# 32 by 32 tiles of k and q for the third token group, its weights and gates worked on inside the first output product: an mLSTM cell with a SwiGLU block on one core

## The chip, the cores and the metric

The kernel runs on one core of one Trainium2 chip. The metric is device time in microseconds of one execution. Engines are named as in the profile: PE (matrix), PEld (its weight loads), DVE (vector), ACT (scalar), POOL (GpSimd), SP (the sync engine, which here issues nearly all DMAs).

## The reference

Two stages follow each other. The first is an mLSTM cell for 4 batches, 8 heads, 768 tokens and a head size of 40, with a running matrix C and vector n for each head:

```python
m_new = np.maximum(f_gate[:, :, t] + m, i_gate[:, :, t])
f_stab = np.exp(f_gate[:, :, t] + m - m_new)
i_stab = np.exp(i_gate[:, :, t] - m_new)
C = f_stab[..., None, None] * C + i_stab[..., None, None] * np.einsum('bhd,bhe->bhde', vt, kt)
n = f_stab[..., None] * n + i_stab[..., None] * kt
h_tilde = np.einsum('bhde,bhe->bhd', C, qt)
denom = np.maximum(np.abs(np.einsum('bhd,bhd->bh', n, qt)[:, :, None]), 1.0)
y[:, :, t] = sigmoid(o_gate[:, :, t]) * h_tilde / denom
```

The second takes the 3072 rows of 320 values (heads side by side) through a SwiGLU block: `(silu(x @ w_gate) * (x @ w_val)) @ w_out`, with 1536 hidden columns. All arrays are float32, and the three weight matrices come as float64.

## The kernel before

The 768 tokens are cut into six groups (g = 0 to 5) of 128 tokens for all 4 batches, which makes 512 rows for the SwiGLU block. The engines run in parallel, and each executes its instructions in the order in which the program text issues them; nothing reorders them. The author therefore interleaves by hand: the long matrix products of group g are issued in chunks, and between the chunks stand the small steps that prepare group g + 1 and load group g + 2. These lists are the dictionaries `slots` (after each chunk of the hidden product) and `after` (after each chunk of the first output product).

**The hidden product** of a group is 12 chunks (`hidden`, L613). A chunk is ten matmuls into two PSUM banks (L618), then silu on ACT (L623) and a product on DVE (L624), which frees the banks. The pool "gen" has four such banks, so PE can be two chunks ahead of L624.

**The output product** of a group multiplies the hidden values by `w_out`. For groups 1 to 5 it goes batch by batch (`project`, L631). For group 0 it goes by chunks of hidden columns through all four banks at once (`project_all`, L637, matmuls on L641), because `w_out` is still being converted from float64: each two chunks of it are made by ACT (L186, L188), DVE (L195, L196) and an addition on POOL (L203). `convert(14)` to `convert(17)` stand in `after`. When the last chunk is done, ACT copies the four banks to `z_sb` (L628), which has two buffers, and SP stores each (L629).

**The cell** for a group needs k and q with the head dimension on partitions (`kT`, `qT`). Groups 1 and 2 load tokens on partitions (`load`, L113), transpose on PE (`turn`, L287 and L292; 64 transposes for a group) and copy out of PSUM on ACT and DVE (L117, L119). Groups 3 to 5 load 32 by 32 tiles (`load_squares`, L305, 16 DMAs for q and 16 for k, rows of 32 or 8 values) into zeroed tiles `q_sq` (a view of `q_sb`) and `k_sq`, and DVE transposes these tiles in place of PE (`turn_squares`, L314). k with tokens on partitions (`k_sb`) is wanted in any case, for the state's update (`add`, L343).

The **weights** of a group start as a load of running maxima to `w_sb` (L421). Then DVE subtracts (`weights_sub`, L425), POOL masks (`weights_mask`, L430, two instructions for each half P of the heads), and ACT exponentiates (`weights_exp`, L434). POOL multiplies them into v (`weigh_values`, L337). The **output gates** are a sigmoid on ACT (`sig`, L437). Exponential, sigmoid and silu each need a table load on ACT when one follows another.

Where this is for the third group (n = 2), before the change: loads of v, k, q and o stand after chunks 1 and 3 of the first output product, subtraction and masks after chunks 8 and 9, the exponentials, sigmoids and `weigh_values` behind the whole product (so behind the four z copies on ACT), and the transposes after chunks 0 and 1 of the hidden product of group 1. The buffers "raw" (two, from the pool `conv`) hold the float64 weights; the pool is closed after the first output product, and `k_sq` takes over its space.

Of the kernel before, what the change touches and what calls it, by code (L numbers as in the profile page):

```python
# [9 lines left out]
F32 = mybir.dt.float32  # L10
# [8 lines left out]
L = 128  # L19
# [5 lines left out]
def kernel(  # L25
# [18 lines left out]
    nc = tc.nc  # L44
# [5 lines left out]
    PP = BH // 2  # L50
# [6 lines left out]
    NKC = DM // HP  # L57
# [13 lines left out]
    conv = early_scope.enter_context(tc.tile_pool(name="conv", bufs=2))  # L71
# [10 lines left out]
    def heads(P):  # L82
        return slice(P * UH, (P + 1) * UH)

    k_sb = const.tile([128, BH, DP], F32)
    q_sb = const.tile([128, BH, DP], F32)
    v_sb = const.tile([128, BH, D1], F32)
    o_sb = const.tile([128, BH, D], F32)
    w_sb = const.tile([128, BH, SUB], F32)
    vw_sb = const.tile([128, BH, D1], F32)  # L90
    kT = const.tile([128, PP, L], F32)
    qT = const.tile([128, PP, L], F32)
# [210 lines left out]
    SQ = 32  # L303

    def load_squares(dst, a, c):  # L305
        for two in range(2):
            for s in range(2):
                r = slice((2 * two + s) * SQ, (2 * two + s + 1) * SQ)
                w = min(SQ, D - s * SQ)
                for t in range(L // SQ):  # L310
                    nc.sync.dma_start(out=dst[r, :, t, 0:w],
                                      in_=a[:, two:H:2, ds(c * L + t * SQ, SQ), ds(s * SQ, w)].rearrange("b h p d -> p (b h) d"))

    def turn_squares(src, dst):  # L314
        for P in range(2):
            a = slice(P * UA, (P + 1) * UA)
            nc.vector.transpose(out=dst[:, a].rearrange("p a t -> p (a t)"), in_=src[:, a].rearrange("p a t d -> p (a t d)"))

    q_sq = q_sb.rearrange("p (a x) d -> p a (x d)", x=2).rearrange("p a (t d) -> p a t d", d=SQ)
# [16 lines left out]
    def weigh_values(eng, P):  # L336
        eng.tensor_tensor(vw_sb[:, heads(P)], v_sb[:, heads(P)], w_sb[:, heads(P), last].to_broadcast([128, UH, D1]),  # L337
                          op=ALU.mult)
# [84 lines left out]
    def weights_sub(n, P):  # L423
        gb = g_T[:, n, heads(P)].unsqueeze(2).to_broadcast([128, UH, SUB])
        nc.vector.tensor_tensor(w_sb[:, heads(P)], gb, w_sb[:, heads(P)], op=ALU.subtract)  # L425

    def weights_mask(P):
        for i in range(2):
            w = w_sb[half(i), heads(P)]
            nc.gpsimd.affine_select(w, w, compare_op=ALU.is_ge, fill=NEG, base=0, pattern=[[0, UH], [1, SUB]],  # L430
                                    channel_multiplier=-1)

    def weights_exp(P):
        nc.scalar.activation(w_sb[:, heads(P)], w_sb[:, heads(P)], AF.Exp)  # L434

    def sig(P):
        nc.scalar.activation(o_sb[:, heads(P)], o_sb[:, heads(P)], AF.Sigmoid)  # L437
# [10 lines left out]
    A, V, G = nc.scalar, nc.vector, nc.gpsimd  # L448
# [164 lines left out]
    def hidden(g, m, first=()):  # L613
        ps = [bank("gv_ps", "gen") for _ in range(2)]
        x = xT(g)
        for kc in range(NKC):
            for i in range(2):
                nc.tensor.matmul(ps[i], lhsT=wgv_sb[half(i), m, PAIRS[kc][i], :], rhs=x[half(i), kc, :],  # L618
                                 start=(kc == 0), stop=(kc == NKC - 1))
        for f in first:  # L620
            f()
        sg = work.tile([128, TW], F32, name="sg")
        nc.scalar.activation(sg, ps[0], AF.Silu)  # L623
        nc.vector.tensor_tensor(hid(g, m), sg, ps[1], op=ALU.mult)  # L624
# [6 lines left out]
    def project(g, u):  # L631
        p = bank("o_ps", "gen")[:, 0:DM]
        for m in range(NFC):
            nc.tensor.matmul(p, lhsT=hid(g, m)[:, ts(u, L)], rhs=wo_sb[:, m, :], start=(m == 0), stop=(m == NFC - 1))  # L634
        result(g, u, p)

    def project_all(g, after):  # L637
        ps = [bank("o_ps", "gen")[:, 0:DM] for _ in range(B)]
        for m in range(NFC):
            for u in range(B):  # L640
                nc.tensor.matmul(ps[u], lhsT=hid(g, m)[:, ts(u, L)], rhs=wo_sb[:, m, :], start=(m == 0),  # L641
                                 stop=(m == NFC - 1))
            for f in after.get(m, ()):
                f()
        for u in range(B):
            result(g, u, ps[u])

    live = {}
# [30 lines left out]
    def load_all(dst, a, n):  # L679
# [3 lines left out]
    run = lambda f, *a: (lambda: f(*a))  # L683
# [6 lines left out]
    slots = {  # L690
        0: [run(first_state, 1, A), run(load_all, k_sb, k, 1), run(load_all, q_sb, q, 1)],
        1: [run(late_maxima), run(piece_load, 6, h_sb[:, NH - NKC:])],
        2: [run(weights_load, 1), run(load_all, v_sb, v, 1), run(decay_rows)],
        3: [run(late_turns)],
        4: [run(decay)],
        5: [run(turn, 0, (A, A), (A, V))],
        6: [run(turn, 1, (A, A), (A, V)), run(piece_load, 7)],
        7: [run(weights_sub, 1, 0), run(weights_sub, 1, 1), run(weights_mask, 0), run(weights_mask, 1)],
        8: [run(weights_exp, 0), run(weights_exp, 1), run(weigh_values, G, 0), run(weigh_values, G, 1),
            run(piece_load, 8)],  # L700
        9: [run(do_scores), run(do_weigh, 0), run(do_weigh, 1), run(load_all, o_sb, o_gate, 1)],
        10: [run(do_add), run(do_state, 2, 0), run(do_state, 2, 1)],
        11: [run(do_attend, 1, 0), run(do_gather, 1, 0, False), run(piece_load, 9)],
    }
    for m in range(NFC):
        hidden(0, m, [run(convert, j, V if j in on_vector else None) for j in ahead[m]])
        for f in slots.get(m, ()):
            f()
    after = {
        0: [run(do_attend, 1, 1), run(convert, 14), run(sig, 0), run(sig, 1), run(do_gate, 0)],  # L710
        1: [run(do_gather, 1, 1), run(weights_load, 2), run(load_all, v_sb, v, 2)],
        2: [run(do_divide, 0), run(convert, 15)],
        3: [run(do_divide, 1), run(load_all, k_sb, k, 2), run(load_all, q_sb, q, 2), run(load_all, o_sb, o_gate, 2)],
        4: [run(convert, 16), run(seam, 1, 0, (A, V, A, V))],
        5: [run(seam, 1, 1, (A, V, A, V))],
        6: [run(convert, 17)],
        8: [run(weights_sub, 2, 0), run(weights_mask, 0)],
        9: [run(weights_sub, 2, 1), run(weights_mask, 1)],
    }
    project_all(0, after)  # L720
    weights_exp(0)
    weights_exp(1)
    sig(0)
    sig(1)
    weigh_values(G, 0)
    weigh_values(G, 1)
    early_scope.close()
    late = ctx.enter_context(tc.tile_pool(name="late", bufs=1))
    xTs.append(late.tile([128, NKC, TW], F32, name="xT1"))
# [1 line left out]
    k_sq = late.tile([128, PP, L // SQ, SQ], F32, name="k_sq")  # L731
# [3 lines left out]
    for g in range(1, NG):  # L735
        n, f = g + 1, g + 2
        slots = {m: [] for m in range(NFC)}
        if n < NG:
            slots[0] = [run(turn, 0, (A, V), (A, V))] if n == 2 else [run(turn_squares, q_sq, qT)]
            slots[1] = [run(turn, 1, (A, V), (A, V))] if n == 2 else [run(turn_squares, k_sq, kT)]  # L740
            if n == 2:
                slots[1].append(run(nc.gpsimd.memset, q_sb, 0.0))
            slots[3] = [run(do_scores), run(do_weigh, 0)]
            slots[4] = [run(do_weigh, 1)]
            slots[5] = [run(do_add), run(do_state, 2 * n, 0)]
            slots[6] = [run(do_state, 2 * n, 1)]
            slots[7] = [run(do_attend, n, 0), run(do_gather, n, 0)]
            slots[8] = [run(do_divide, 0)]
            slots[9] = [run(do_attend, n, 1), run(do_gather, n, 1)]
            slots[10] = [run(do_divide, 1), run(seam, n, 0, (A, V, A, V))]  # L750
            slots[11] = [run(seam, n, 1, (A, V, A, V))]
        if f < NG:
            slots[2] += [run(load_squares, q_sq, q, f), run(load_squares, k_sq, k, f)]
            slots[5].append(run(load_all, k_sb, k, f))
            slots[9] += [run(load_all, v_sb, v, f), run(weights_load, f)]
            slots[10].append(run(load_all, o_sb, o_gate, f))
        for m in range(NFC):
            hidden(g, m)
            for s in slots[m]:
                s()  # L760
        for u in range(B):
            if f < NG and u < 2:
                weights_sub(f, u)
                weights_mask(u)
            if f < NG and u == 2:
                weights_exp(0)
                weights_exp(1)
                sig(0)
                sig(1)
                weigh_values(nc.gpsimd, 0)  # L770
                weigh_values(nc.gpsimd, 1)
            project(g, u)
# [30 lines left out]
```

## Time and profile before

| | |
|---|---|
| median of three runs | 572.78 us (571.49 to 572.90) |
| profiled execution | 572.01 us, span 570.2 us |
| PE busy | 559.7 us (98%), granted clock 0.997 |
| DVE, ACT, POOL busy | 219.5, 144.3, 106.1 us |
| first output product on PE (L641) | 102.5 to 133.1 us |
| hidden product of group 1 (L618) | 133.1 to 198 us, with other work between |
| DMA | 39.81 MB, 168219 packets, of which 158728 under 512 B |

The span is the profiled part of the execution; the execution's own time has about 1.8 us around it. Times of single instructions count from the start of the span. A row of a timeline has start, length, engine, line, what is written and read, how many instructions were merged, and in brackets the idle time just before and who ended it.

### The profile page before, as it was taken

The page shows a single profiled execution, that of the slowest core. Times are in us where ns is not written, and L with a number is a line of the kernel's source. Part 1 is how long each engine was busy: PE and PEld are TensorE (multiplying, and loading weights), DVE is VectorE, ACT ScalarE, POOL GpSimd, SP SyncE. Part 2 cuts the span into 40 slices and gives each one's busy share as a digit, 9 for nine tenths or more (in the row PEclk, how much of TensorE's full clock was granted, in tenths as well). Part 3 has the DMA queues.
Part 4 walks back from the last instruction along what each step waited for, and adds up shares of the span by engine and source line. Part 5 has one row for each costly group of instructions (what it writes and reads, how often), then busy time and mean ns, then how long its engine had stood idle before and what let it go on. Part 6 is the DMA issues. An engine that isn't in the chain of part 4 may idle for free.

```text
span 570.2 us, 11868 instructions
## 1 busy us (share of the span) xinstructions
PE 559.7 (98%) x5215; PEld 328.4 (58%) x5216; DVE 219.5 (38%) x379; ACT 144.3 (25%) x224; POOL 106.1 (19%) x103
## 2 busy tenths in 40 slices
PE   8997999999999999999999999999999999999997
PEld 4856545765555576455576455567455567544475
DVE  5776576970425520434620434630433630011100
ACT  4365456436201214111115110114211020111100
POOL 2132344464111132011132001232001200000000
PEclk9999999999999999999999999999999999999999
DMA  9999991593472810454630355450000000000000
GB/s 124 179 271 193 173 265 45 134 146 82 48 83 36 140 28 25 46 67 53 109 48 23 49 58 66 77 85 23 13 2 2 2 1 34 13 0 1 0 24 23
DMA packets 168219, 39.81 MB, mean 70 GB/s; under 512 B 158728, under 2 KB 163336, under 8 KB 168168
## 3 DMA queue, kind: packets, MB, share of 16 engines
q1 hardware_dynamic: 165588, 34.89, 38.0%
q10 hardware_dynamic: 2580, 4.16, 3.3%
q8 instruction: 41, 0.67, 0.5%
q14 instruction: 10, 0.08, 0.1%
HBM read 35.03 MB, written 4.01 MB: 68 GB/s over the span
## 4 chain that ended last, share of the span: by engine, by line
PE 84%; DMA 5%; SPq 3%; ACT 3%; DVE 3%; POOL 1%; issue 1%; ACTq 0%; DVEq 0%; POOLq 0%
PE gv_ps L618 49%; PE o_ps L634 23%; PE o_ps L641 4%; SPq L113 3%; DMA raw<-in_moe_w_val_dram 3%; PE intra L372 2%; PE inter L367 2%; DMA raw<-in_moe_w_gate_dram 2%; PE sp L327 1%; PE add L348 1%; PE tp_x L413 1%; DVE wgv_sb L196 1%; DVE wgv_sb L195 1%; POOL C L357 1%; PE tp_kq L292 0%
## 5 line engine op out<-in xcount | busy, mean ns | idle before, releaser
L618 PE MATMUL gv_ps<-xT,wgv_sb 64*128 64x512 f32 x1440 | 321.6, 596 | 3.8 <-POOL wgv_sb L203 2.9
L618 PEld LDWEIGHTS gv_ps<-xT,wgv_sb 64*128 64x128 f32 x1440 | 144.2, 188 | 156.3 <-issue 148.1
L624 DVE TENSOR_TENSOR h_sb<-sg,gv_ps 128x512 f32<-128x512 f32 x72 | 49.5, 688 | 289.2 <-ACT sg L623 273.9
L634 PE MATMUL o_ps<-wo_sb,h_sb 128*128 128x320 f32 x480 | 130.5, 433 | 0.0
L634 PEld LDWEIGHTS o_ps<-wo_sb,h_sb 128*128 128x128 f32 x480 | 90.8, 190 | 38.2 <-issue 0.8
L623 ACT ACTIVATE sg<-gv_ps 128x512 f32<-128x512 f32 x72 | 43.0, 598 | 261.4 <-PE gv_ps L618 261.4
L357 POOL TENSOR_TENSOR C<-C,dec 128x328 f32<-128x328 f32 x20 | 14.5, 738 | 150.3 <-DVE C L359 150.3
L628 ACT COPY z_sb<-o_ps 128x320 f32<-128x320 f32 x24 | 10.2, 426 | 114.1 <-PE o_ps L634 102.7
L430 POOL TENSOR_SCALAR_AFFINE_SELECT w_sb<-w_sb 64x1024 f32<-64x1024 f32 x20 | 28.2, 1408 | 26.1 <-DVE w_sb L425 25.1
L641 PE MATMUL o_ps<-wo_sb,h_sb 128*128 128x320 f32 x96 | 26.9, 437 | 0.0
L393 POOL TENSOR_TENSOR o_sb<-o_sb,y_sb 128x640 f32<-128x640 f32 x10 | 14.2, 1425 | 48.5 <-DVE y_sb L384 48.5
L641 PEld LDWEIGHTS o_ps<-wo_sb,h_sb 128*128 128x128 f32 x96 | 17.9, 190 | 7.2
L384 DVE TENSOR_TENSOR y_sb<-y_sb,intra 64x328 f32<-64x328 f32 x40 | 19.7, 493 | 0.9
L337 POOL TENSOR_TENSOR vw_sb<-v_sb,w_sb 128x656 f32<-128x656 f32 x10 | 12.9, 1316 | 31.3 <-issue 29.4
L203 POOL TENSOR_TENSOR wgv_sb<-wgv_sb,low 128x640 int32<-128x640 int32 x8 | 13.3, 1668 | 28.5 <-DVE wgv_sb L196 28.5
L367 PEld LDWEIGHTS inter<-C,qT 64*64 64x64 f32 x640 | 10.2, 134 | 7.3 <-issue 6.1
L359 DVE TENSOR_TENSOR C<-C,add 128x328 f32<-128x328 f32 x20 | 9.9, 494 | 10.5 <-POOL C L357 10.5
L425 DVE TENSOR_TENSOR w_sb<-g_T,w_sb 128x1024 f32<-128x1024 f32 x10 | 13.1, 1352 | 0.0
L203 POOL TENSOR_TENSOR wo_sb<-wo_sb,low 128x640 int32<-128x640 int32 x6 | 10.2, 1708 | 15.0 <-DVE wo_sb L196 10.5
L334 DVE TENSOR_TENSOR w_sb<-sp,w_sb 128x512 f32<-128x512 f32 x20 | 12.7, 683 | 0.0
L372 PE MATMUL intra<-v_sb,w_sb 64*64 64x41 f32 x640 | 12.3, 228 | 0.4 <-DVE C L359 0.3
L186 ACT ACTIVATE top<-raw 128x640 f32<-128x640 f32 x12 | 9.6, 800 | 11.5 <-issue 5.3
(126 smaller groups left out, 371.2 us busy)
## 6 DMA issues: line engine op xcount, KB each, us to landing
w_sb<-M_dram SPq DMA_DIRECT2D x10, 512.0 KB, 6.4
k_sb<-in_k_dram SPq DMA_DIRECT2D x12, 320.0 KB, 6.2
v_sb<-in_v_dram SPq DMA_DIRECT2D x12, 320.0 KB, 7.0
o_sb<-in_o_gate_dram SPq DMA_DIRECT2D x12, 320.0 KB, 7.1
raw<-in_moe_w_out_dram SPq DMA_DIRECT2D x3, 1280.0 KB, 8.3
out_dram<-z_sb SPq DMA_DIRECT2D x24, 160.0 KB, 1.8
q_sb<-in_q_dram SPq DMA_DIRECT2D x6, 320.0 KB, 8.8
q_sb<-in_q_dram SPq DMA_DIRECT2D x24, 64.0 KB, 2.2
```

What stands on the lines that cost most here:

```text
L113: nc.sync.dma_start(out=dst[:, heads(P), 0:D], in_=tokens(a, c, P))
L203: (eng or nc.gpsimd).tensor_tensor(dst, dst, lo, op=ALU.add)
L357: nc.gpsimd.tensor_tensor(state(s + 1)[:, a], state(s)[:, a], dec[:, s - 2, a].unsqueeze(2).to_broadcast([128, UA, D1]), op=ALU.mult)
L367: nc.tensor.matmul(inter[two][half(i), a, :], lhsT=qT[half(two), P * UA + a, half(i)], rhs=state(2 * n + i)[half(two), P * UA + a, :], sta ...
L372: nc.tensor.matmul(intra[i][half(c), a, :], lhsT=w_sb[half(i), h, :], rhs=v_sb[half(i), h, :], start=True, stop=True)
L384: nc.vector.tensor_tensor(t, t, intra[i][half(c)], op=ALU.add)
L430: nc.gpsimd.affine_select(w, w, compare_op=ALU.is_ge, fill=NEG, base=0, pattern=[[0, UH], [1, SUB]], channel_multiplier=-1)
L618: nc.tensor.matmul(ps[i], lhsT=wgv_sb[half(i), m, PAIRS[kc][i], :], rhs=x[half(i), kc, :], start=(kc == 0), stop=(kc == NKC - 1))
L623: nc.scalar.activation(sg, ps[0], AF.Silu)
L624: nc.vector.tensor_tensor(hid(g, m), sg, ps[1], op=ALU.mult)
L634: nc.tensor.matmul(p, lhsT=hid(g, m)[:, ts(u, L)], rhs=wo_sb[:, m, :], start=(m == 0), stop=(m == NFC - 1))
L641: nc.tensor.matmul(ps[u], lhsT=hid(g, m)[:, ts(u, L)], rhs=wo_sb[:, m, :], start=(m == 0), stop=(m == NFC - 1))
```

## The change

For group 2, k and q are loaded as 32 by 32 tiles and transposed by DVE, as for groups 3 to 5. The memset of `q_sb` moves from group 1's hidden product to chunk 7 of group 0's, and the 16 DMAs of q's tiles to chunk 10, ahead of the last piece of `w_out`. The tiles of k go to a "raw" buffer, which POOL clears after chunk 3 of the first output product; their 16 DMAs follow `o_sb`'s load on SP, and `k_sb`'s load comes behind them, after chunk 7. DVE transposes q's tiles after chunk 8 and k's after chunk 11. `weights_sub` and `weights_mask` move from after chunks 8 and 9 to after chunks 5 and 7, around `convert(17)`. `weights_exp` and `weigh_values` move to after chunk 9 and `sig` to after chunk 10, so that on ACT they stand ahead of the four z copies. From group 1's hidden product the 64 PE transposes and their 8 copies go.

```diff
-        7: [run(weights_sub, 1, 0), run(weights_sub, 1, 1), run(weights_mask, 0), run(weights_mask, 1)],
+        7: [run(weights_sub, 1, 0), run(weights_sub, 1, 1), run(weights_mask, 0), run(weights_mask, 1),
+            run(nc.gpsimd.memset, q_sb, 0.0)],
...
-        10: [run(do_add), run(do_state, 2, 0), run(do_state, 2, 1)],
+        10: [run(do_add), run(do_state, 2, 0), run(do_state, 2, 1), run(load_squares, q_sq, q, 2)],
...
+    def early_squares(part):
+        if part == 0:
+            live["k_sq"] = conv.tile([128, 4 * NKC * 128], F32, name="raw")[:, 0:PP * L].rearrange("p (a t d) -> p a t d", a=PP, d=SQ)
+            nc.gpsimd.memset(live["k_sq"], 0.0)
+            load_squares(live["k_sq"], k, 2)
+        else:
+            turn_squares(live.pop("k_sq"), kT)
+
     after = {
...
-        3: [run(do_divide, 1), run(load_all, k_sb, k, 2), run(load_all, q_sb, q, 2), run(load_all, o_sb, o_gate, 2)],
+        3: [run(do_divide, 1), run(load_all, o_sb, o_gate, 2), run(early_squares, 0)],
         4: [run(convert, 16), run(seam, 1, 0, (A, V, A, V))],
-        5: [run(seam, 1, 1, (A, V, A, V))],
+        5: [run(seam, 1, 1, (A, V, A, V)), run(weights_sub, 2, 0), run(weights_mask, 0)],
         6: [run(convert, 17)],
-        8: [run(weights_sub, 2, 0), run(weights_mask, 0)],
-        9: [run(weights_sub, 2, 1), run(weights_mask, 1)],
+        7: [run(weights_sub, 2, 1), run(weights_mask, 1), run(load_all, k_sb, k, 2)],
+        8: [run(turn_squares, q_sq, qT)],
+        9: [run(weights_exp, 0), run(weights_exp, 1), run(weigh_values, G, 0), run(weigh_values, G, 1)],
+        10: [run(sig, 0), run(sig, 1)],
+        11: [run(early_squares, 1)],
     }
     project_all(0, after)
-    weights_exp(0)
-    weights_exp(1)
-    sig(0)
-    sig(1)
-    weigh_values(G, 0)
-    weigh_values(G, 1)
     early_scope.close()
...
-            slots[0] = [run(turn, 0, (A, V), (A, V))] if n == 2 else [run(turn_squares, q_sq, qT)]
-            slots[1] = [run(turn, 1, (A, V), (A, V))] if n == 2 else [run(turn_squares, k_sq, kT)]
-            if n == 2:
-                slots[1].append(run(nc.gpsimd.memset, q_sb, 0.0))
+            if n > 2:
+                slots[0] = [run(turn_squares, q_sq, qT)]
+                slots[1] = [run(turn_squares, k_sq, kT)]
```

## The prediction

> **What bounds the kernel now.** The first lines to read on the page are busy time and the chain that ended last.
>
> ```profile
> PE 559.7 (98%) x5215; PEld 328.4 (58%) x5216; DVE 219.5 (38%) x379; ACT 144.3 (25%) x224; POOL 106.1 (19%) x103
> ...
> PE 84%; DMA 5%; SPq 3%; ACT 3%; DVE 3%; POOL 1%; issue 1%; ACTq 0%; DVEq 0%; POOLq 0%
> ```
>
> PE is busy 98% of the span and carries 84% of the chain. An instruction taken off PE is time off the end, unless PE then waits for somebody. So I read PE's own timeline at the place of the change, the step from the first output product (L641) to the hidden product of group 1 (L618).
>
> ```profile
> 133.07 4.56 PE L618 MATMUL gv_ps<-xT,wgv_sb 64*128 64x512 f32 x20
> 137.47 0.66 PE L292 MATMUL tp_kq<-ident,k_sb 64*128 64x64 f32 x16
> 137.96 0.67 PE L292 MATMUL tp_kq<-ident,q_sb 64*128 64x64 f32 x16
> 138.46 4.51 PE L618 MATMUL gv_ps<-xT,wgv_sb 64*128 64x512 f32 x20
> 143.35 0.27 PE L292 MATMUL tp_kq<-ident,k_sb 64*128 64x64 f32 x1 [0.38 <-ACT kT L117]
> 143.84 0.71 PE L292 MATMUL tp_kq<-ident,k_sb 64*128 64x64 f32 x15 [0.22 <-ACT qT L117]
> 144.80 0.71 PE L292 MATMUL tp_kq<-ident,q_sb 64*128 64x64 f32 x15 [0.25 <-DVE qT L119]
> 145.29 8.86 PE L618 MATMUL gv_ps<-xT,wgv_sb 64*128 64x512 f32 x40
> ```
>
> [...]The L641 matmuls end and L618 starts at 133.07 with no gap. From there to 145.29 are 12.2 us with two chunks of L618; two chunks alone take 8.8 (145.29 to the next product at 154.07). The 64 transposes cost the other **3.4 us**, waits included.
>
> Next, ACT around that seam (its timeline):
>
> ```profile
> 131.56 0.96 ACT L628 COPY z_sb<-o_ps 128x320 f32<-128x320 f32 x2 [9.47 <-PE o_ps L641]
> 133.94 0.98 ACT L628 COPY z_sb<-o_ps 128x320 f32<-128x320 f32 x2 [1.41 <-DMA out_dram<-z_sb]
> 134.94 1.28 ACT L434 ACT_TABLE_LOAD   x1
> 136.23 2.00 ACT L434 ACTIVATE w_sb<-w_sb 128x1024 f32<-128x1024 f32 x2
> 138.25 1.28 ACT L437 ACT_TABLE_LOAD   x1
> 139.55 1.36 ACT L437 ACTIVATE o_sb<-o_sb 128x640 f32<-128x640 f32 x2
> ```
>
> The four z copies empty the four "gen" PSUM banks. The first pair frees the banks of the first L618 chunk, at 132.5, before PE wants them at 133.1; the second pair frees those of the second chunk, and waits for the first stores, because z_sb has two buffers. Exponentials and sigmoids come after. Last, DVE and POOL just before (two timelines):
>
> ```profile
> 122.68 3.70 DVE L425 TENSOR_TENSOR w_sb<-g_T,w_sb 128x1024 f32<-128x1024 f32 x2
> ```
>
> ```profile
> 118.33 1.55 POOL L203 TENSOR_TENSOR wo_sb<-wo_sb,low 128x640 int32<-128x640 int32 x1 [0.86 <-DVE wo_sb L196]
> 122.91 2.38 POOL L203 TENSOR_TENSOR wo_sb<-wo_sb,low 128x640 int32<-128x640 int32 x1 [3.04 <-DVE wo_sb L196]
> 125.25 5.75 POOL L430 TENSOR_SCALAR_AFFINE_SELECT w_sb<-w_sb 64x1024 f32<-64x1024 f32 x4
> ```
>
> The two subtractions, 1.22 us each when alone (78.04), take 3.70, and the addition takes 2.38 instead of 1.55: they stretch each other. The masks end at 131.0.
>
> **What the Trainium skill says.** *SBUF — State Buffer*, "Who interferes with whom": a VectorE instruction with two SBUF inputs contends with a GpSimd one that reads SBUF, not with one that only writes; the later one is held until the earlier is done. The trace agrees twice: the lengths just named, and the memset L271 on POOL (36.83, 0.62 us), which ran unstretched beside a two-input L272 subtraction. *ScalarE: Activation LUTs*, "What ACT_TABLE_LOAD costs": 1.28 us for a load plus 1.38 of drain. The trace has 1.28 and the next activation at once (134.94, 136.23), so I use 1.28. *DMA: Bandwidth & Descriptors*, "Queues, rings and completion order": each DMA engine takes descriptors in ring order, so a store issued behind a load queues behind it. The trace fits: the store issued after o_sb's load had drained landed in 1.8 us, against 7.1 for the load.
>
> **The change, part by part.**
>
> *Off PE:* 64 transposes (L292), −3.4 us as above. With them go 4 ACT copies (0.59 each) and 4 DVE copies (0.68), inside that stretch, no further gain.
>
> *DVE transposes:* four at 1.22 us (L317 row), 4.9 us. DVE is idle 16.5 us before its L624 at 142.86, which hides them; without that cover they would delay L624 and so the banks. q's pair runs from about 126.4. k's pair needs the squares, about 131.5, and ends by 134; the first L624 is due only after 139. 0 us.
>
> *Memset of q_sb and 16 q DMAs, moved into hidden chunks 7 and 10:* on POOL 1.80 us behind the masks, 86.1 to about 88.2, ahead of L337 (88.00): 0.2 late, ended by 91, and the product that reads it starts at 93.4. On SP the squares take 8.6 to 9.7 us (their rows at 147.40 and 156.05), 88.3 to 97–98, ahead of the last w_out piece, which SP could not issue before 96.69 anyhow (it waits for ACT's L188). At most 1.3 late, landing by about 106; its first reader is at 114.84. 0 us.
>
> *Memset of the k buffer and 16 k DMAs:* the memset (1.80) enters POOL behind the copy L400, 117.5 to 119.3, ahead of L203 of the fifth w_out block, now 120.9; PE needs it at chunk 8, about 124.3 (119.95 plus two chunks of 2.2). 0 us. On SP, o_sb now comes first (115 to 119.3), then the squares to about 129, k_sb's two loads to 133. In DMA work the squares replace q_sb's two loads: about 0.64 busy for 9 us, near 6, against some 6 (a fifth of the stage's 30 share-us in the windows table from 108 to 138). So the queue should drain at about the old time, and the z stores find it nearly empty.
>
> *Weights and gates before the z copies:* this is the part that can cost. On ACT two table loads, two exponentials and two sigmoids now stand **ahead** of the z copies, and they wait for POOL's masks. I walk the chain, with the durations that these instructions show when one holds the other up. The seam's copies on DVE end at 120.9. First subtraction to 122.1; L195 (0.49) to 122.6; mask (1.05) to 123.6; L196 (0.6) to 124.2; mask to 125.3; second subtraction (1.1) to 126.4; L203 of the last w_out block (1.4) to 127.8 (PE needs it at 128.7, slack 0.9); two more masks (2.35) to 130.1; second exponential (1.05) to 131.2; table 132.5; sigmoids (1.36) 133.8; two z copies (0.96) 134.8. PE wants the banks at 133.1, so it waits **1.7 us**. Bounds: with no holding up, the masks end at 128.3, the sigmoids at 132.0, the z copies at 133.0: 0 us. With every instruction at its full length on top of the holding, 2.1, and 3.3 if memsets held the lock as well. I take 1.7.
>
> *The next wait:* the first stores go out at about 134.5 and land by 136.3 to 138.0; z copies three and four end by 138.5, and PE's second chunk wants them at 134.8 + 4.4 = 139.2. 0 us, slack 0.7. Behind them on ACT stand L623's table load, to 139.8, and the first silu, to 140.4; DVE frees the first pair of banks by 141.1, and PE's third chunk wants them at 143.6.
>
> Sum: −3.4 + 1.7 = −1.7 us on an execution of 572.0 (span 570.2 and 1.8 around it). The median of the three runs is 572.8, 0.8 above; from it, **571.1**.
>
> **The rivals.** A difference under 0.3% (1.7 us) is about what a measurement of this kernel cannot tell from none; my forecast lies on that edge.
>
> *The chain is hidden.* If masks and subtractions overlap better than I assume, ACT is through by 133 and the whole 3.4 counts: 569.4. For it: uncontended masks take 1.14. Against it: the 3.70 and 2.38 rows.
>
> *The lock bites further.* L203 of the last block comes after 128.7 and memsets hold DVE too: PE waits 3 to 5 instead of 1.7, giving 572.4 to 574.4. Against it: L271 beside L272.
>
> *Slower: the stores queue behind the squares.* 8192 small descriptors go into the stage where the DMA share is 1.0 to 1.5 (110 to 128). If they take twice their quiet 9.7 us, they end at 138.8, k_sb at 142.9, the first stores land at 144.7, the z copies end at 145.7, and PE's second chunk waits 6.5 us from 139.2: 572.8 − 3.4 + 1.7 + 6.5 = 577.6. It starts to cost when the first store lands after 138.7, undoes the gain at 140.4, and is slower by over 0.3% from 142.1. Against it: the equal DMA work worked out above.
>
> That the change doesn't act isn't among them: in the changed program's order PE has no transposes left in group 1, and ACT has the sigmoids ahead of the z copies.
>
> **How the numbers follow.** Forecast 0.45 (570.3 to 572.1), hidden chain 0.22 (569.3 to 570.3), longer lock 0.13, slower by the stores 0.20 (574.5 to 577.6). Faster by over 0.3% takes the second and 0.18 of the first: 0.40. Slower takes the last and 0.01 of the lock: 0.21. The rest is 0.39. Eight in ten: from 569.3, where the whole saving counts, up to 574.8, past the lock case.
>
> **What would show it.** L618 chunks 0 to 3 of group 1 should follow each other without L292. The gap between L641's end and L618 should be 1 to 2.5 us, its releaser ACT's z copy; no gap means the hidden chain. Masks on POOL should end near 130, sigmoids near 134. A PE gap after the first chunk, ended by z copies that wait for their stores, is the slower rival. I am wrong if a gap stands elsewhere, at chunk 10 of L641 (last block late) or near 88 to 98.

## The result, and the profile after

The changed kernel takes 569.83 us (median of 19 runs, 566.21 to 572.75); the kernel before, beside it on the same chip, 572.33 us (19 runs, 569.67 to 574.39). The ratio is 0.9959, with a 95% interval of 0.994 to 0.9978: **0.41% faster, 2.3 us**, between 1.3 and 3.4. The forecast was 571.1 us, a gain of 1.7 on a median of 572.8.

The profiled execution took 570.14 us (span 568.4). Its busy times, and its chain by engine (a q marks an engine's own queue of instructions or DMAs):

```profile
PE 557.4 (98%) x5151; PEld 328.5 (58%) x5152; DVE 222.1 (39%) x379; ACT 142.1 (25%) x220; POOL 107.7 (19%) x104
...
PE 83%; DMA 5%; SPq 4%; DVE 2%; POOL 2%; ACT 2%; issue 1%; ACTq 0%; POOLq 0%; DVEq 0%
```

PE lost 64 instructions and 2.3 us of busy time, and still leads the chain. Where it went is in PE's timeline around the seam, the step from L641 to L618:

```profile
103.59 2.42 PE L641 MATMUL o_ps<-wo_sb,h_sb 128*128 128x320 f32 x8
...
121.03 13.19 PE L641 MATMUL o_ps<-wo_sb,h_sb 128*128 128x320 f32 x48
135.06 17.76 PE L618 MATMUL gv_ps<-xT,wgv_sb 64*128 64x512 f32 x80 [0.84 <-ACT z_sb L628]
152.74 2.10 PE L327 MATMUL sp<-qT,kT 64*64 64x64 f32 x128
```

Four chunks of L618 follow each other without a transpose between them. Ahead of them is something new: PE idles 0.84 us until a z copy of ACT frees its bank.

Both traces reach this place at different times, for a reason outside the change (the last section). So I measure the **stage** inside each trace, from the first matmul of L641 to the first of the scores (L327). Its two ends before:

```profile
102.51 2.42 PE L641 MATMUL o_ps<-wo_sb,h_sb 128*128 128x320 f32 x8
...
154.07 2.10 PE L327 MATMUL sp<-qT,kT 64*64 64x64 f32 x128
```

Before it is 102.51 to 154.07, or 51.56 us; after, 103.59 to 152.74, or 49.15. The stage is 2.4 us shorter, as much as the runs say. It splits in two: the seam's L618 chunks, with what stands between them, take 17.7 in place of 21.0 (133.07 to 154.07), so **−3.3**; and L618 starts 31.5 us after the stage's start in place of 30.6, so **+0.9**. What follows the stage takes 415.5 to 416.1 us in all ten traces, this pair and the eight experiments below, so nothing of size is hidden there.

ACT's timeline shows why L618 starts late:

```profile
126.18 1.06 ACT L434 ACTIVATE w_sb<-w_sb 128x1024 f32<-128x1024 f32 x1 [1.73 <-POOL w_sb L430]
130.96 1.06 ACT L434 ACTIVATE w_sb<-w_sb 128x1024 f32<-128x1024 f32 x1 [3.73 <-POOL w_sb L430]
132.03 1.28 ACT L437 ACT_TABLE_LOAD   x1
133.33 1.36 ACT L437 ACTIVATE o_sb<-o_sb 128x640 f32<-128x640 f32 x2
134.60 0.73 ACT L628 COPY z_sb<-o_ps 128x320 f32<-128x320 f32 x2
137.57 0.82 ACT L628 COPY z_sb<-o_ps 128x320 f32<-128x320 f32 x2 [2.25 <-DMA out_dram<-z_sb]
```

The second exponential waits for POOL's masks, which end at 130.9. Behind it a table load and two sigmoids stand ahead of the z copies, which could have run from about 132.6. The second pair of copies waits for the first stores; it comes at 137.6, before PE wants those banks (135.06 + 4.4 = 139.5). DVE and POOL in the stage (two timelines):

```profile
127.14 2.36 DVE L317 STREAM_TRANSPOSE qT<-q_sb 128x1024 f32<-128x1024 f32 x2
132.41 2.37 DVE L317 STREAM_TRANSPOSE kT<-raw 128x1024 f32<-128x1024 f32 x2 [2.91 <-POOL vw_sb L337]
140.33 0.69 DVE L624 TENSOR_TENSOR h_sb<-sg,gv_ps 128x512 f32<-128x512 f32 x1 [5.55 <-ACT sg L623]
```

```profile
118.50 1.80 POOL L713 MEMSET raw<- 128x2048 f32 x1
...
126.23 2.40 POOL L203 TENSOR_TENSOR wo_sb<-wo_sb,low 128x640 int32<-128x640 int32 x1
128.57 2.36 POOL L430 TENSOR_SCALAR_AFFINE_SELECT w_sb<-w_sb 64x1024 f32<-64x1024 f32 x2
```

The DVE transposes are done at 134.8 and their next neighbour starts at 140.3: they are hidden. The last `w_out` block is ready at 128.6; PE's chunk 10 starts at 121.03 + 4 × 2.2 = 129.8.

### The profile page after: what moved, and what is told of

Read it like the earlier page. It is cut to its first block, busy times and chain, and to the rows that moved or that the text cites. A ratio compares the mean times of both kernels' runs of the same rounds, so it can differ in the third digit from the quotient of the medians.

```text
span 568.4 us, 11784 instructions
## 1 busy us (share of the span) xinstructions
PE 557.4 (98%) x5151; PEld 328.5 (58%) x5152; DVE 222.1 (39%) x379; ACT 142.1 (25%) x220; POOL 107.7 (19%) x104
## 4 chain that ended last, share of the span: by engine, by line
PE 83%; DMA 5%; SPq 4%; DVE 2%; POOL 2%; ACT 2%; issue 1%; ACTq 0%; POOLq 0%; DVEq 0%
PE gv_ps L618 50%; PE o_ps L634 23%; SPq L113 3%; DMA raw<-in_moe_w_val_dram 3%; PE o_ps L641 2%; DMA h_sb<-in_moe_w_gate_dram 2%; PE intra L372 2%; PE inter L367 2%; PE sp L327 1%; PE add L348 1%; PE tp_x L413 1%; POOL w_sb L430 1%; DVE w_sb L425 1%; SPq L161 1%; POOL C L357 1%
## 5 line engine op out<-in xcount | busy, mean ns | idle before, releaser
L618 PE MATMUL gv_ps<-xT,wgv_sb 64*128 64x512 f32 x1440 | 321.4, 596 | 5.7 <-POOL wgv_sb L203 4.1
L618 PEld LDWEIGHTS gv_ps<-xT,wgv_sb 64*128 64x128 f32 x1440 | 146.5, 188 | 157.3 <-issue 141.8
L624 DVE TENSOR_TENSOR h_sb<-sg,gv_ps 128x512 f32<-128x512 f32 x72 | 49.5, 687 | 281.7 <-ACT sg L623 266.5
L641 PE MATMUL o_ps<-wo_sb,h_sb 128*128 128x320 f32 x96 | 26.9, 437 | 0.0
L641 PEld LDWEIGHTS o_ps<-wo_sb,h_sb 128*128 128x128 f32 x96 | 17.9, 190 | 7.2
L203 POOL TENSOR_TENSOR wgv_sb<-wgv_sb,low 128x640 int32<-128x640 int32 x8 | 13.4, 1670 | 29.6 <-DVE wgv_sb L196 29.6
L337 POOL TENSOR_TENSOR vw_sb<-v_sb,w_sb 128x656 f32<-128x656 f32 x10 | 12.8, 1304 | 23.2 <-issue 23.0
L367 PEld LDWEIGHTS inter<-C,qT 64*64 64x64 f32 x640 | 10.2, 134 | 7.3 <-issue 6.1
L372 PE MATMUL intra<-v_sb,w_sb 64*64 64x41 f32 x640 | 12.3, 228 | 0.4 <-DVE C L359 0.3
L387 DVE TENSOR_SCALAR den<-den 128x16 f32<-128x16 f32 x10 | 12.3, 1227 | 0.3
```

Of the source, the lines that this page charges most:

```text
L367: nc.tensor.matmul(inter[two][half(i), a, :], lhsT=qT[half(two), P * UA + a, half(i)], rhs=state(2 * n + i)[half(two), P * UA + a, :], sta ...
L372: nc.tensor.matmul(intra[i][half(c), a, :], lhsT=w_sb[half(i), h, :], rhs=v_sb[half(i), h, :], start=True, stop=True)
```

## The experiments

The theory: the saving is PE's transposes (3.3 us), the cost is z copies that stand behind ACT's chain (0.9 us). Rivals: the saving comes from ACT's order; the gap comes from another wait; the tiles' DMAs cost something. The stages, measured as above, and the runs:

| kernel | stage us | against before | ratio of runs, 95% interval |
|---|---|---|---|
| before | 51.56 | | |
| after | 49.15 | −2.41 | 0.9959 (0.994 to 0.9978) |
| e1 tiles only | 55.20 | +3.64 | 1.0041 (1.0019 to 1.0063) |
| e2 weights and gates only | 51.23 | −0.33 | 0.9996 (0.9975 to 1.0017) |
| e3 sigmoids between z copies | 48.21 | −3.35 | 0.9933 (0.9906 to 0.9961) |
| e4 sigmoids first | 48.02 | −3.54 | 0.9927 (0.9903 to 0.995) |
| e5 no k tiles | 49.40 | −2.16 | 0.9939 (0.9915 to 0.9962) |
| e6 k tiles twice | 58.79 | +7.23 | 1.0108 (1.0071 to 1.0145) |
| e7 e1, k_sb late | 49.83 | −1.73 | 0.9946 (0.9928 to 0.9964) |
| e8 e1, gap filled | 52.46 | +0.90 | 1.0012 (0.9988 to 1.0036) |

The median of before beside e1 to e4 was 572.42 us, beside e5 to e8 571.97. The intervals are about 0.2 to 0.4% to each side, so for differences of a microsecond I go by the stage of the trace, and the runs only say whether it is plausible. Each stage is one execution; up to the end of L641, ahead of the seam, equal work differs by up to 0.3 us from trace to trace. For e7 the stage's gain lies outside the interval of the runs, which say more, and for e5 at its edge; what makes that difference is not known.

**e1: the tiles alone.**

```diff
-        9: [run(weights_exp, 0), run(weights_exp, 1), run(weigh_values, G, 0), run(weigh_values, G, 1)],
-        10: [run(sig, 0), run(sig, 1)],
...
     project_all(0, after)
+    weights_exp(0)
+    weights_exp(1)
+    sig(0)
+    sig(1)
+    weigh_values(G, 0)
+    weigh_values(G, 1)
```

> Of the change, only the tiles and the earlier subtractions and masks: exponentials, sigmoids and weigh_values stand behind the z copies again, as before. Theory (the saving is PE's transposes, the cost is the z copies that stand behind ACT's chain): no PE gap between L641 and L618, but ACT then works through z copies, exponentials, two table loads and sigmoids before the first silu, as in the trace before, where L624 freed the first banks about 10.5 us after L618 began (133.07 to 143.5). PE's first two chunks take 8.8, so it waits about 1.7 us ahead of chunk 2. Sum -3.3 + 1.7 = -1.6 us against before, 0.7 slower than the change. Rival (ACT's order does not matter, the weights have slack): -3.3 us, faster than the change.

It was slower than before by 2.3 us, 3.6 in the stage. The seam has no gap, as the theory says, but then (PE, ACT):

```profile
131.30 9.01 PE L618 MATMUL gv_ps<-xT,wgv_sb 64*128 64x512 f32 x40
143.65 12.36 PE L618 MATMUL gv_ps<-xT,wgv_sb 64*128 64x512 f32 x40 [3.34 <-ACT sg L623]
155.94 2.09 PE L327 MATMUL sp<-qT,kT 64*64 64x64 f32 x128
```

```profile
134.90 0.81 ACT L628 COPY z_sb<-o_ps 128x320 f32<-128x320 f32 x2 [4.14 <-DMA out_dram<-z_sb]
```

Two things were not in my sum. PE idles 3.3 us, twice what I worked out: z copies three and four waited 4.14 us for stores, where they had waited 1.41 before. And chunks 2 and 3 take 12.3 us in place of 8.8. For the slow chunks, the table of windows for e1 (stretch, its length, busy time of PE, PEld, DVE, ACT and POOL, granted clock, DMA share, GB/s) has a candidate:

```profile
131.00:140.30 9.30, 9.30 (x42) 5.17 (x40) 1.17 (x2) 5.36 (x6) 2.10 (x2) 1.00 0.88 136
140.30:143.60 3.30, 0.01 (x1) 0.00 (x0) 0.00 (x0) 3.26 (x6) 2.90 (x3) 0.94 0.69 82
...
145.00:147.00 2.00, 2.00 (x6) 0.93 (x4) 0.00 (x0) 0.00 (x0) 0.00 (x0) 0.50 0.65 77
147.00:149.00 2.00, 2.00 (x8) 1.12 (x6) 0.00 (x0) 0.00 (x0) 0.00 (x0) 0.50 0.72 82
149.00:151.00 2.00, 2.00 (x9) 1.21 (x8) 0.00 (x0) 0.00 (x0) 0.00 (x0) 0.74 0.63 67
151.00:153.00 2.00, 2.00 (x12) 1.17 (x10) 0.69 (x1) 0.60 (x1) 0.00 (x0) 1.00 0.76 93
```

Near the end of the idle stretch PE's granted clock falls to 0.50, and it comes back at about 150. Both readings became questions for e7 and e8.

**e2: weights and gates alone.** k and q keep their rows and PE transposes.

```diff
-        3: [..., run(load_all, k_sb, k, 2), run(load_all, q_sb, q, 2), run(load_all, o_sb, o_gate, 2)],
+        3: [..., run(load_all, o_sb, o_gate, 2), run(load_all, k_sb, k, 2), run(load_all, q_sb, q, 2)],
...
-        5: [run(seam, 1, 1, (A, V, A, V))],
+        5: [run(seam, 1, 1, (A, V, A, V)), run(weights_sub, 2, 0), run(weights_mask, 0)],
...
-        8: [run(weights_sub, 2, 0), run(weights_mask, 0)],
-        9: [run(weights_sub, 2, 1), run(weights_mask, 1)],
+        7: [run(weights_sub, 2, 1), run(weights_mask, 1)],
+        9: [run(weights_exp, 0), run(weights_exp, 1), run(weigh_values, G, 0), run(weigh_values, G, 1)],
+        10: [run(sig, 0), run(sig, 1)],
...
     project_all(0, after)
-    weights_exp(0)
-    weights_exp(1)
-    sig(0)
-    sig(1)
-    weigh_values(G, 0)
-    weigh_values(G, 1)
```

> Of the change, only the earlier weights and gates; k and q keep their row layout and the 64 PE transposes stay (o_sb is loaded ahead of k_sb and q_sb, so that the sigmoids have their input). Theory: the same gap of about 0.9 us between L641 and L618 as with the change; the transposes stay, but ACT is free for their copies, so they cost about 2.0 us (64 at 31 ns from start to start) in place of 3.4. Sum +0.9 - 1.4 = -0.5 us against before. Rival (the saving comes from ACT's order and not from the tiles): -2 us or more.

No difference in the runs, −0.33 in the stage. On PE:

```profile
133.78 4.88 PE L618 MATMUL gv_ps<-xT,wgv_sb 64*128 64x512 f32 x20 [0.83 <-ACT z_sb L628]
```

The same gap, without a single tile: the wait belongs to ACT's order. From there to the scores (153.56) are 19.8 us, 2.2 more than four chunks (17.6), so the transposes cost 2.2 instead of 3.4 once the exponentials and sigmoids were out of the way of their copies. The rival (all of the saving from ACT's order) falls.

**e3 and e4: the sigmoids out of the z copies' way.** e3 moves them between the second and the third z copy:

```diff
-        10: [run(sig, 0), run(sig, 1)],
...
         for u in range(B):
             result(g, u, ps[u])
+            if u == 1:
+                sig(0)
+                sig(1)
```

> The change, with the sigmoids and their table load moved between the second and the third z copy. Theory: the second exponential ends at about 132.0 on the clock of the changed kernel's trace, the first two z copies by 133.0, before L641 ends at 134.2: the gap of 0.84 us goes. The last two z copies end near 136.6, the second chunk wants them at 138.6. Sum about -0.9 us against the change, -3.3 against before. Rival (the gap is not the z copies but another wait, POOL's masks or the conversion of w_out): the gap stays.

e4 puts them ahead of the exponentials:

```diff
-        9: [run(weights_exp, 0), run(weights_exp, 1), run(weigh_values, G, 0), run(weigh_values, G, 1)],
-        10: [run(sig, 0), run(sig, 1)],
+        9: [run(sig, 0), run(sig, 1), run(weights_exp, 0), run(weights_exp, 1), run(weigh_values, G, 0), run(weigh_values, G, 1)],
```

> The change, with the sigmoids ahead of the exponentials on ACT; since the sigmoid's table is still the active one there, the load ahead of them falls away, and one for the exponentials stays. Theory: the sigmoids run while ACT waits for the masks (it idles 1.7 and 3.7 us there), if o_sb has landed by about 126; the second exponential ends at about 132.0 as before, the z copies by 133.0, and the gap goes: -0.9 us against the change, -3.3 against before. Rival (the exponential, not what stands behind it, is what holds the z copies): the gap stays near 0.8.

Both remove the gap, and both stages are about 1 us shorter than the change's. PE in e3:

```profile
134.17 17.72 PE L618 MATMUL gv_ps<-xT,wgv_sb 64*128 64x512 f32 x80
```

PE and ACT in e4:

```profile
117.76 13.19 PE L641 MATMUL o_ps<-wo_sb,h_sb 128*128 128x320 f32 x48
130.88 17.54 PE L618 MATMUL gv_ps<-xT,wgv_sb 64*128 64x512 f32 x80
```

```profile
119.77 0.74 ACT L437 ACTIVATE o_sb<-o_sb 128x640 f32<-128x640 f32 x1
120.72 0.74 ACT L437 ACTIVATE o_sb<-o_sb 128x640 f32<-128x640 f32 x1 [0.21 <-DMA o_sb<-in_o_gate_dram]
...
127.70 1.06 ACT L434 ACTIVATE w_sb<-w_sb 128x1024 f32<-128x1024 f32 x1 [3.73 <-POOL w_sb L430]
129.37 0.96 ACT L628 COPY z_sb<-o_ps 128x320 f32<-128x320 f32 x2 [0.62 <-PE o_ps L641]
134.43 0.80 ACT L628 COPY z_sb<-o_ps 128x320 f32<-128x320 f32 x2 [4.09 <-DMA out_dram<-z_sb]
```

The masks hold the second exponential as before (3.73 us), and the z copies now wait for PE and not PE for them. The sigmoids run without a table load: the last one on ACT ahead of them is the one for the sigmoids of the group before. **e3 and e4 are the best versions**, 0.67 and 0.73% under before (medians 567.66 and 567.81 us against 572.42); the runs cannot tell them apart. The slack of e4 is thin: the second pair of z copies starts at 134.43, and PE wants the banks at 130.88 + 4.4 = 135.3.

**e5: no tiles of k.** The DMAs of k's tiles are left out.

```diff
             nc.gpsimd.memset(live["k_sq"], 0.0)
-            load_squares(live["k_sq"], k, 2)
```

> The change without the 16 DMAs of k's tiles for group 2 (the k of that group's scores is then zero; the memset and all else stay). Theory (the tiles' DMAs and their place on SP are hidden): the stores of z land sooner, but PE's gap between L641 and L618 stays at 0.8 us and nothing else moves: within 0.3 us of the change. Rival (SP or the DMA queue already holds up the z copies or the transposes): the time falls by more than 0.5 us.

```profile
135.19 17.76 PE L618 MATMUL gv_ps<-xT,wgv_sb 64*128 64x512 f32 x80 [0.84 <-ACT z_sb L628]
```

The gap is 0.84 and the four chunks take 17.7, as in the change. The stage is 0.25 longer, nearly all of it in the attention product L372 (1.75 us against 1.51), ahead of the seam: the tiles' DMAs are hidden. The runs' ratio is 0.2% lower than the change's, with intervals that overlap; the trace shows nothing in the stage that would answer to it. The last two z copies waited 1.63 in place of 2.25.

**e6: tiles of k twice.**

```diff
             load_squares(live["k_sq"], k, 2)
+            load_squares(live["k_sq"], k, 2)
```

> The change with the 16 DMAs of k's tiles issued twice, which puts 10.2 us more on SP and the DMA queue ahead of k_sb's load and the stores of z. Theory (the slower rival of the prediction, with its price): on the clock of the changed kernel's trace the squares end at 140.7, k_sb at 142.5, the first store is issued then and lands near 145, z copies three and four end by 146, and PE waits ahead of its second chunk from 139.5 to about 145.4: 6 us more. If an idle PE of that length also loses its clock, as in the run with the tiles only, another 3 to 4 us: 6 to 10 us slower than the change. Rival (stores do not queue behind loads, or there is more slack): less than 2 us.

578.26 us; the stage is 9.6 longer than the change's. PE, then ACT:

```profile
144.75 15.68 PE L618 MATMUL gv_ps<-xT,wgv_sb 64*128 64x512 f32 x60 [6.83 <-ACT z_sb L628]
```

```profile
144.27 0.81 ACT L628 COPY z_sb<-o_ps 128x320 f32<-128x320 f32 x2 [10.96 <-DMA out_dram<-z_sb]
```

The prediction's slower rival is real, with the price it was given (6.5 us of waiting; here 6.8). SP was issuing loads until it could issue the first store at 139.23, some 6 us after the first z copies had ended; the store then took until 144.2 to land, behind `k_sb`'s load. On top comes the clock, 0.50 from about 142.7 to 149.5 (windows as for e1):

```profile
141.00:143.00 2.00, 0.00 (x0) 0.00 (x0) 0.45 (x1) 0.00 (x0) 1.49 (x1) 0.92 1.52 146
...
147.00:149.00 2.00, 2.00 (x7) 1.62 (x5) 0.69 (x1) 0.00 (x0) 0.00 (x0) 0.50 0.84 120
149.00:151.00 2.00, 2.00 (x10) 1.67 (x9) 0.00 (x0) 0.00 (x0) 0.00 (x0) 0.87 0.56 32
```

The change stays clear of this because its tiles are issued in 10.2 us, here 18.9.

**e7: e1 with k_sb's load behind the stores.** (The edit is against e1.)

```diff
-        7: [run(weights_sub, 2, 1), run(weights_mask, 1), run(load_all, k_sb, k, 2)],
+        7: [run(weights_sub, 2, 1), run(weights_mask, 1)],
...
     project_all(0, after)
+    load_all(k_sb, k, 2)
```

> The run with the tiles only, with k_sb's load issued behind the stores of z in place of ahead of them. Theory (3.34 us of PE's idle time there are 1.6 from ACT's row of exponentials and sigmoids and about 1.8 from z copies that wait for stores queued behind k_sb's load; the clock falls because PE idles that long): the last two z copies come about 2 us sooner, PE's gap ahead of chunk 2 shrinks to 1.3 to 2 us. With the clock kept, about -1.6 us against before; if 1.6 us of idle PE is already enough to lose the clock, about +1.5 us. Rival (stores do not queue behind the load): the gap stays at 3.3 us and the time at +2.3 us.

```profile
134.80 0.95 ACT L628 COPY z_sb<-o_ps 128x320 f32<-128x320 f32 x2 [1.41 <-DMA out_dram<-z_sb]
```

```profile
143.71 9.57 PE L618 MATMUL gv_ps<-xT,wgv_sb 64*128 64x512 f32 x40 [0.92 <-ACT sg L623]
```

The stores' wait is 1.41 again, as before the change. The third z copy started 4.7 us after SP had issued the first store in e1 (130.24 to 134.90), and 1.9 us after it here (132.87 to 134.80), so it is not SP that was late in e1: the store itself took longer behind the load. PE idles 0.92 and then some 0.7 more inside chunk 2, which takes 9.5 us with chunk 3: its first bank is free after silu, its second only after L624 (0.69). That is the 1.6 of the sum, and the stage moved by −1.73 where −1.6 was expected (the runs say −3.1, with an interval of 1 us to each side). So e1's excess was stores queued behind a load, and what that gap did to the clock. With this one load moved, the tiles alone gain about as much as the whole change: −1.73 against −2.41 in the stage, 0.9946 against 0.9959 in the runs.

**e8: e1 with PE kept busy in the gap.** (The edit is against e1.)

```diff
+    def fill():
+        t = bank("fill")[:, 0:DM]
+        for m in range(5):
+            nc.tensor.matmul(t, lhsT=wo_sb[:, m, 0:128], rhs=wo_sb[:, m, :], start=True, stop=True)
...
+            if n == 2:
+                slots[1] = [fill]
```

> The run with the tiles only, with five matmuls of 320 columns into a spare bank (nobody reads them) behind the second chunk of group 1, 2.75 us of work in PE's gap of 3.34. Theory (the gap costs itself and then 3.5 us more, because the granted clock is at 0.50 for some 6 us after it): PE's remaining gap is about 0.6 us, the clock stays at 1.00, chunks 2 and 3 take 8.8 us in place of 12.3: -3.5 us against the tiles only, about -1.2 us or less against before. Rival (chunks 2 and 3 are slow for another reason, such as L624 or DMA traffic): they still take about 12 us, and the time stays at +2.3 us.

```profile
139.96 2.96 PE L748 MATMUL fill<-wo_sb 128*128 128x320 f32 x10
143.37 9.57 PE L618 MATMUL gv_ps<-xT,wgv_sb 64*128 64x512 f32 x40 [0.45 <-ACT sg L623]
```

```profile
144.00:146.00 2.00, 2.00 (x11) 1.48 (x11) 0.64 (x2) 0.00 (x0) 0.00 (x0) 1.00 0.57 44
146.00:148.00 2.00, 2.00 (x12) 1.53 (x10) 0.00 (x0) 0.04 (x1) 0.00 (x0) 1.00 0.84 117
```

Useless matmuls make the stage shorter: chunks 2 and 3 take 9.5 us and the clock stays at 1.00 in every window from 132 to 158. That makes the clock the cause of e1's slow chunks and settles the rival. Against e1 the stage is 2.7 shorter, not 3.5, since 0.7 of the slow chunks was the wait for L624 just named. (In the runs the step from e1 to e8 is 1.0041 to 1.0012, with intervals that overlap.) My −1.2 against before took the 3.5 from e1's +2.3 in the runs; in the stage it is 3.64 − 2.74, or +0.9.

## Why the prediction was right

**PE's transposes, −3.4:** measured −3.3. Right, and e2 shows that 1.2 of it was waiting for the copies out of PSUM, which stood behind ACT's other work.

**The seam's wait, +1.7:** measured +0.9. The mechanism is right (e2 has it without tiles, e3 and e4 without sigmoids in the way lose it), but the term was mis-sized. On the clock of the trace before (1.08 subtracted) the chain's steps are:

| end of | predicted | measured |
|---|---|---|
| last w_out block (L203) | 127.8 | 127.6 |
| masks | 130.1 | 129.9 |
| second exponential | 131.2 | 130.9 |
| sigmoids | 133.8 | 133.6 |
| first, second z copy | 134.3, 134.8 | 134.0, 134.3 |
| L618 starts | 134.8 | 134.0 |

The walk through DVE and POOL, which hold each other up, came out within 0.25 us. What was mis-sized is the last step: I let PE wait for both z copies, but its first matmul needs one bank only (it starts at 135.06, when the pair of copies, 134.60 to 135.33, is half done), and I charged 0.96 for a pair that in the trace before had itself been waiting for PE; free-running it takes 0.73.

**What was costed at nothing** was nothing: the memset of q_sb ran in 2.03 us behind the masks and L337 started 0.26 late by the same clock; q's tiles left SP at 98.1 (97 to 98 predicted), k's at 129.5; the DVE transposes ran where they were placed, from 126.1 and 131.3; z copies three and four came at 136.5, inside 136.3 to 138.0. e5 confirms the DMAs.

**The rivals.** The hidden chain (569.3 to 570.3) did not happen as such, although the median lies in that range: the gap is there. The longer lock did not happen: the last `w_out` block was ready 1.2 us before PE's need of it, and the memsets took 1.80 and 2.03 us. The slower rival needs more DMA work than the change has (e6).

**The total** was −1.7, measured −2.3 by the runs and −2.4 by the stage; the difference is the 0.8 of the seam's wait, less 0.1 on the transposes. In absolute time before also measured 0.5 lower (572.33, not 572.8), so the median of 569.83 lies below the forecast's own band, in that of a rival whose mechanism is absent. The runs alone, with a gain between 1.3 and 3.4, hardly tell the two apart; the trace's 0.84 us of idle PE does.

What the prediction did not see is what the transposes were covering. They kept PE busy while ACT was behind, and without them PE meets the next wait. In e1 that is 1.6 us of ACT's order (e7), and then stores behind `k_sb`'s load and the clock, which make the tiles alone slower than before. The change escapes the second wait because its order on ACT lets the first silu start sooner, 4.6 us after L618 against 11.7 in e1; e7 escapes most of it by moving one load. Weights and gates alone gain nothing to be measured (e2).

## What to carry to other kernels

When work is taken off the bounding engine, ask what that work was covering: in e1 the next wait (3.3 us, for banks) came out at once, and with the clock cost more than the transposes had. ACT here did its instructions in program order, so put the one that frees a bank ahead of everything nobody waits for yet; moving two sigmoids was worth 1 us of the stage. Issue stores that release a buffer ahead of loads that are needed only later (e7 against e1). No run puts e7's late load into e3 or e4, where it might widen the slack.

## What the runs showed of the hardware that I had not expected

PE's granted clock. After 3.3 us without matmuls (e1), and 6.8 us (e6), it fell to 0.50 and stayed there for about 6.8 us in both, though PE was busy again for most of it. That cost 2.8 us in e1 (chunks 2 and 3 in 12.3 against 9.5 in e8) and 2.4 in e6 (three chunks in 15.6 against 13.2). Gaps of 0.84 and 0.92 us (after, e7) left it at 1.00.

The same happens in both kernels before the change's place: at 50 to 60 us PE waits for POOL's L203 on the gate weights, 2.87 us before and 4.08 after, and the granted clock of that stretch is 0.83 and 0.66 (PE's line and the window, before and then after):

```profile
54.63 6.50 PE L618 MATMUL gv_ps<-xT,wgv_sb 64*128 64x512 f32 x20 [2.87 <-POOL wgv_sb L203]
50.00:60.00 10.00, 7.13 (x32) 5.29 (x30) 6.72 (x14) 6.67 (x9) 3.28 (x3) 0.83 1.21 134
...
55.58 6.63 PE L618 MATMUL gv_ps<-xT,wgv_sb 64*128 64x512 f32 x20 [4.08 <-POOL wgv_sb L203]
50.00:60.00 10.00, 5.92 (x26) 3.85 (x24) 6.14 (x14) 6.63 (x9) 3.08 (x2) 0.66 1.24 139
```

No line of the change stands there. Over the ten traces this wait is 1.3 to 4.5 us, and its length alone does not decide: after 1.53 us (e2) and 2.87 (before) the clock was lost, after 2.24 (e6) and 2.73 (e4) it was not. How long it then stays at 0.50 has two values. It is about 3.4 us in five traces (before, e2, e3, e5, e7), where PE was at work when the clock fell, or 0.2 us later. It is about 6.8 in three (after, here; e1 and e6 in the stage), where PE idled on for 0.4 to 2.9 us. The Trainium skill, *TensorE: Matmul & The Clock Gate*, "What's actually happening", describes two states of the clock, full and half, switched by activity over windows of about 3.4 us; the two values agree, and the two durations are one and two such windows. No run here varies a gap alone, so what decides is not shown.

The four traces that keep the clock at this place reach the stage at 100.3 to 101.6 us, the six that lose it at 102.3 to 103.6. It is a likely cause of the runs' scatter of some 6 us, which no experiment here tested.
